# Per-tile first K and Q groups, small weights first on a second ring, and a landing margin for weight pieces, in a one-core attention and gated-MLP kernel

## The chip, the core and the metric

The kernel runs on one core of a Trainium2 chip. The metric is device time in microseconds (us) of one execution. Engines are called as in the profile: PE (matrix products; PEld is its loading of weights), ACT (activations), DVE (vector work), POOL, and SP, which here only issues DMA transfers. ACT can issue transfers too; the transfers of SP and of ACT go through two rings to the same 16 DMA engines.

## The reference

One transformer block on x of 2048 tokens by 1024 features, bf16:

```python
h  = x + A(layernorm(x))       # attention: 32 query heads of 32, one shared K and V head
h2 = h + B(layernorm(h))       # gated MLP, inner width 3584
# A: q = x@wq (1024x1024), k = x@wk, v = x@wv (1024x32 each)
#    o = softmax(q k^T / sqrt(32)) v ; o @ wo (1024x1024)
# B: (sigmoid(x@w_gate) * (x@w_up)) @ w_down
```

## The kernel before, in words

**A plan written at build time.** Every instruction is an `Op` (L22) with an engine, dependencies, a planned occupation and latency and a priority. `Plan` (L39 to L121) is a list scheduler: for each of ACT, DVE, POOL and SP it keeps a heap and a time `free`, and puts the ready op of best priority next (`step`, L79). A transfer (an op with `nbytes`) is planned to start 1.4 us after its issue or when the one before it has ended, to move 280 bytes per ns, and to land 0.9 us later (L99 to L102). PE's order is made by the main loop (L974 to L1044), which looks at the planned time `t` and chooses among score blocks, PV blocks and groups in `queues`, in the order of `PRIO` (L388). The plan's times exist only at build time; what is left in the program is the order of each engine's instructions, with semaphore waits. An engine that waits for one instruction holds up all behind it. The launch line and the helpers stand in several rows of the profile: L391 is every matrix product, L282 and L283 are copies out of PSUM on ACT and DVE.

**Stages.** 16 tiles of 128 tokens. x is loaded by SP (`load_x`, L296), pairs of tiles get their layer norm on DVE and POOL (`stats`, L326; centring L371, scaling L378), and the result is transposed: tiles 0 and 1 on PE (`mk_xT`, L417, copied out by ACT), the others by transposing transfers on SP (`dma_xT`, L439). From the transposed tiles PE makes K and V (`mk_KV`, L467) for each pair of tiles, and Q (`mk_Q`, L503) for each of 8 groups of 128 columns. K's weights are first repeated four times across columns by ACT (`rep_ops`, L322), so that K comes out in four row groups. w_k and w_v are loaded by ACT's ring (L311, L312), after x of tile 1 has landed in the plan. Q of the first two tiles goes to `QTb`; Q of the others goes through DRAM and comes back a tile at a time.

**Attention.** A *visit* (G, kq) is one pair of Q groups for one query tile (G counts them, four to a tile) against 256 keys (kq, 0 to 7). `emit_S` (L608) issues 8 score products into the PSUM tile `S_ps` (six banks, three pairs used in turn), and ACT takes exp of them in two instructions of 1024 columns (L631). The order is the list `visits` (L571 to L573): for the first four G in pairs of G through kq 0 to 3, then kq 4 to 7, then G by G. Each visit takes two of the 20 slots `Pr` (four of which lie in `wo_sb`); they come free once the PV block of four visits (`mk_PV`, L680) is done. PV, sums of the exponentials (L665, DVE) and the output projection (`mk_OP`, L788) follow.

**MLP.** For every tile: second layer norm, a transposing transfer of `hn` to `hnT` (L818), 14 gate and up groups (`mk_GU`, L880, 8 products of 512 columns each), tanh on ACT, product on DVE, a transposing transfer to `hact` (L917), and two down groups of 28 products (`mk_D`, L932). Gate and up weights don't fit: they are streamed in *pieces* of 256 KB (`load_piece`, L862) into 22 slots `ring`, again for every tile, with slots still held being reused. `pump` (L264) releases pieces to SP no faster than `PACE` bytes per ns once visit 120 is passed. A group is started only when its pieces are issued and, in the plan, its first two have landed (L926, L927).

**Filling.** Before the first visit PE runs products of the identity with zeros into `S_ps` bank 5 (L1034) to keep busy; later, when nothing is ready, products of `ident` with `kT4` (L1041), which show as F_ps<-kT,ident.

Of the kernel before, what the change touches and what calls it, by code (L numbers as in the profile page):

```python
# [13 lines left out]
P = 128  # L14
DH = 32
LN_EPS_BF16 = 1.0013580322265625e-05
SEM = 75.0
AHEAD = 200.0
PMAX = 1


# [17 lines left out]
class Plan:  # L39
# [3 lines left out]

    def __init__(self):
        self.lists = {e: [] for e in ("pe",) + self.ENG}
        self.free = {e: 0.0 for e in ("pe",) + self.ENG}
        self.heap = {e: [] for e in self.ENG}
        self.dma_free = collections.Counter()
        self.seq = 0
# [29 lines left out]
    def step(self, limit):  # L79
        best = None  # L80
        for e in self.ENG:
            h = self.heap[e]
            if h:
                s = max(self.free[e], min(o.ready for o in h))
                if best is None or s < best[0]:
                    best = (s, e)
        if best is None or (limit is not None and best[0] > limit):
            return False
        s, e = best
        h = self.heap[e]  # L90
        o = min((o for o in h if o.ready <= s + 1e-9), key=lambda o: (o.prio, o.seq))
        if e == "dve" and o.prio >= 3:
            soon = [x for x in h if x.prio <= PMAX and s < x.ready <= s + AHEAD]
            if soon:
                o = min(soon, key=lambda x: x.ready)
                s = o.ready
        h.remove(o)
        self.free[e] = s + o.occ
        if o.nbytes:  # L99
            go = max(s + 1400.0, self.dma_free["sp"])  # L100
            self.dma_free["sp"] = go + o.nbytes / 280.0
            o.end = self.dma_free["sp"] + 900.0  # L102
        else:
            o.end = s + o.lat
        o.pos = len(self.lists[e])
        self.lists[e].append(o)
        for u in o.users:
            u.ready = max(u.ready, o.end)
            u.missing -= 1
            if u.missing == 0:  # L110
                self.heap[u.eng].append(u)
        o.users = []
        return True
# [18 lines left out]
def t_mm(n):  # L132
    return dict(occ=max(25.0, n / 2.4 + 2.7), lat=max(25.0, n / 2.4 + 2.7) + 170.0 + SEM)


def bass_sequential_preLN__grouped_kv_mqa__glu_gated_glu__prompt_kernel(
# [12 lines left out]
    Bsz, S, D = A_x.shape  # L149
# [25 lines left out]
    DPP = 2  # L175
    NPI = DT // DPP
    USES = [(p, w, d) for t, p, w in ITEMS for d in range(NPI)]
    PACE = 205.0
    xf = A_x[0]
    of = out[0]  # L180

    with ExitStack() as es:
# [43 lines left out]
        def xnT(dt, a, n):  # L226
            return xnT4[a // 512][:, dt, a % 512:a % 512 + n]
# [24 lines left out]
        def dma(fn, key, nbytes, deps=(), prio=5, ring="sp", occ=520.0):  # L252
            return pl.op(ring, fn, deps, occ=occ, key=key, nbytes=nbytes, prio=prio)
# [19 lines left out]
        def evac(fn_act, fn_dve, n, deps, prio, dve_rate=0.96):  # L273
            now = pl.free["pe"]
            a = max(pl.free["act"], now) + sum(o.occ for o in pl.heap["act"]) + n / 1.2
            d = max(pl.free["dve"], now) + sum(o.occ for o in pl.heap["dve"]) + n / dve_rate
            if a + (2000.0 if v else 0.0) < d:
                return pl.op("act", fn_act, deps, prio=prio, **t_act(n))
            return pl.op("dve", fn_dve, deps, prio=prio, **t_dve(n, dve_rate))

        def both(out_ap, in_ap):
            return (lambda: ACT.activation(out=out_ap, in_=in_ap, func=ACTF.Copy),  # L282
                    lambda: DVE.tensor_copy(out=out_ap, in_=in_ap))  # L283
# [12 lines left out]
        def load_x(ts, deps=()):  # L296
            sl = slice(ts[0] * P, (ts[-1] + 1) * P)
            o = dma(lambda: SP.dma_start(x_sb[:, ts[0]:ts[-1] + 1, :], xf[sl, :].rearrange("(a p) n -> p a n", p=P)),
                    f"x{ts[0]}", P * D * 2 * len(ts), deps, prio=0)
            for t in ts:  # L300
                x_ld[t] = o

        def load_wq(a, b, deps=()):
            o = dma(lambda: SP.dma_start(wq2[a // 4][:, :, a % 4 * P:(a % 4 + b - a) * P], A_wq[:, a * P:b * P].rearrange("(a p) n -> p a n", p=P)),
                    f"wq{a}", D * P * (b - a) * 2, deps, prio=0)
            for g in range(a, b):
                wq_ld[g] = o

        load_x([0])
        load_x([1])  # L310
        wk_ld = dma(lambda: ACT.dma_start(wk_sb, A_wk.rearrange("(a p) j -> p a j", p=P)), "wk", P * DT * DH * 6, [x_ld[1]], prio=0, ring="act")  # L311
        wv_ld = dma(lambda: ACT.dma_start(wv_sb, A_wv.rearrange("(a p) j -> p a j", p=P)), "wv", P * DT * DH * 6, [x_ld[1]], prio=0, ring="act")  # L312
        load_wq(0, 2)
        load_x([2, 3])
        load_wq(2, 4)
        load_x([4, 5])
        warm = pl.op("act", lambda: ACT.activation(out=tnh[:, 0, 0:1], in_=half, func=ACTF.Exp), [c0], prio=1, occ=1400)

# [41 lines left out]
        xnorm = {}  # L360
        xT_ev = {}
        SCALE_ON = ["dve"] * 16
        for ts in [[t, t + 1] for t in range(0, NT, 2)]:
            sv = stats(0, ts, [x_sb[:, t, :] for t in ts], [[x_ld[t]] for t in ts], 3)
            if ts[0] + 6 < NT:
                load_x([ts[0] + 6, ts[0] + 7], [sv[2]])
            if ts[0] == 0:
                load_wq(4, 8, [sv[2]])
            for t in ts:
                xt, sc = x_sb[:, t, :], rstd[:, 0, t:t + 1]  # L370
                cen = pl.op("dve", lambda t=t, xt=xt: DVE.tensor_scalar(  # L371
                    out=xt, in0=xt, scalar1=mvr[:, 0, t, 0:1], scalar2=None, op0=ALU.subtract),
                    [sv[0]], prio=2, occ=360, lat=560)
                if SCALE_ON[t] == "act":
                    xnorm[t] = pl.op("act", lambda xt=xt, sc=sc: ACT.activation(out=xt, in_=xt, func=ACTF.Copy, scale=sc),
                                     [cen, sv[1]], prio=1, **t_act(1024))
                else:
                    xnorm[t] = pl.op("dve", lambda xt=xt, sc=sc: DVE.tensor_scalar(  # L378
                        out=xt, in0=xt, scalar1=sc, scalar2=None, op0=ALU.mult), [cen, sv[1]], prio=1, occ=360, lat=560)
# [5 lines left out]
                self.cls, self.atoms, self.first, self.after = cls, atoms, first, after  # L385

        queues = collections.defaultdict(collections.deque)
        PRIO = ["xT", "KV", "Q0", "OP", "GU", "D", "Q"]  # L388

        def mm(o, l, r, start, stop, **kw):  # L390
            fn = lambda: PE.matmul(o, lhsT=l, rhs=r, start=start, stop=stop, **kw)  # L391
            if not kw:
                fn.col = lambda: [mm(o[DH * j:DH * (j + 1)], l[:, DH * j:DH * (j + 1)], r, start, stop,
                                     tile_position=(0, DH * j)) for j in range(4)]
            return fn
# [48 lines left out]
            queue_after_xT(t)  # L444

        def queue_after_xT(t):
            if t % 2 == 1:
                for part in (("k", "v") if t == 1 else ("kv",)):
                    queues["KV"].append(mk_KV(t // 2, part))
            if t == 1:  # L450
                for g in range(NG):
                    queues["Q0"].append(mk_Q(g, 0, 256))
            if 1 < t < 8 and t % 2 == 1:
                for g in range(NG):
                    queues["Q"].append(mk_Q(g, (t - 1) * P, 256))
            if t % 4 == 3 and t > 8:
                for g in range(NG):
                    queues["Q"].append(mk_Q(g, (t // 4) * 512, 512))

        k_ev, v_ev = {}, {}  # L460

        q_left = [6 * NG]
        q_left4 = [2 * NG, 2 * NG, NG, NG]
# [104 lines left out]

        tile_last_S = {}

        visits = [(G + i, kq) for G in range(0, NX, 2) for kq in range(VPH) for i in range(2)]  # L571
        visits += [(G, kq) for G in range(NX) for kq in range(VPH, VPG)]
        visits += [(G, kq) for G in range(NX, NT * ND) for kq in range(VPG)]  # L573
        NV = len(visits)
# [8 lines left out]
        def s_ready(v):  # L583
            G, kq = visits[v]
            qb, g = G // ND, 2 * (G % ND)
            if any(g + k not in q_ready[qb] for k in range(2)):
                return None
            if kq not in k_ev:
                return None
            reclaim(v)  # L590
            if len(p_free) < 2:
                return None
            deps = [q_ready[qb][g], q_ready[qb][g + 1], k_ev[kq]]
            if 2 * v - 2 >= 0:
                deps.append(exps[2 * v - 2])
            return deps

        def reclaim(v):
# [375 lines left out]
        while True:  # L974
# [56 lines left out]
            if v == NV and cur is None and not any(queues.values()):  # L1031
                break
            if v == 0 and known([c_id, c_w], t):
                pl.op("pe", mm(S_ps[:, 5, :], ident[:, :], hact[:, 0:512], True, True), [c_id, c_w],  # L1034
                      **t_mm(512 if t > 5200.0 else 1024))
                continue
            idle += 1
            spare = [b for b in range(2) if known(bank_rel[b], t) and (cur is None or b != cur_b)]
# [112 lines left out]
```

The softmax here doesn't subtract the row's maximum and nothing guards it: scores larger than these inputs give would overflow.

## Time and profile before

| what | us |
|---|---|
| median of 7 runs | 1095.05 (1092.92 to 1097.06) |
| the profiled execution, its own time | 1093.38 |
| its span in the profile | 1091.3 |
| PE, ACT, DVE busy in it | 1049.5, 1006.3, 903.8 |
| first exp starts | 18.98 |
| last exp ends | 1022.2 |
| last product on PE | 1088.4 |

A row of the timeline reads: start, length, engine, line, operation, what it writes <- what it reads, shape, count, and in brackets the idle time of the engine before it and what ended it. A row of the page's list of groups ends with the busy time and the mean of one. A row of waits reads: engine, its line, who released it: us in total, times, longest. All durations come from this one profiled execution.

### The profile page before, as it was taken

Reading aid. Unit: us, or ns where it says so; the run is one execution under the profiler, and the core shown is the slowest. Engines: PE = TensorE matmul, PEld = TensorE weight load, DVE = VectorE, ACT = ScalarE, POOL = GpSimd, SP = SyncE. Lnnn points to the kernel's source line nnn. Section 1 sums busy time; section 2 is a strip of 40 time slices with the busy share of each in tenths; the row PEclk is TensorE's granted clock in tenths of the full one; section 3 lists DMA queues with packets and bytes.
Section 4 is the critical chain, followed back from the end, with each engine's and each line's share of the span. In section 5 each row is a group of like instructions: output and inputs, shape, how many; then the busy total and the mean of one; then the engine's idle time right before and its main releaser. Section 6 shows DMA issues by size and latency. Waiting matters only on the chain.

```text
span 1091.3 us, 31052 instructions
## 1 busy us (share of the span) xinstructions
PE 1049.5 (96%) x12601; PEld 480.0 (44%) x12775; DVE 903.8 (83%) x1755; ACT 1006.3 (92%) x1162; POOL 22.8 (2%) x56
## 2 busy tenths in 40 slices
PE   8999999999999999999999999999999999999998
PEld 5664444444444444444444444443444444444443
DVE  8779988898988988898988989898888989798711
ACT  4899999999999999999999999999999999999510
POOL 1100000000000000000000000000000000000000
PEclk9999999999999999999999999999999999999999
DMA  9896499959589696959789685969878595968993
GB/s 256 190 291 203 151 274 276 276 130 268 151 220 240 158 242 148 242 141 252 199 184 255 150 245 145 245 165 234 220 175 237 160 238 140 253 170 206 250 274 106
DMA packets 310990, 228.16 MB, mean 209 GB/s; under 512 B 121920, under 2 KB 302144, under 8 KB 310848
## 3 DMA queue, kind: packets, MB, share of 16 engines
q1 hardware_dynamic: 308768, 226.04, 80.4%
q8 instruction: 101, 1.65, 0.6%
q10 hardware_dynamic: 2080, 0.13, 0.1%
q14 instruction: 41, 0.34, 0.1%
HBM read 195.69 MB, written 7.86 MB: 187 GB/s over the span
## 4 chain that ended last, share of the span: by engine, by line
PE 63%; ACT 23%; issue 5%; DVE 5%; DMA 3%; ACTq 0%; SPq 0%; DVEq 0%
PE F_ps L391 54%; ACT Pr L631 22%; PE S_ps L391 10%; DVE Ts L665 3%; DMA zone<-in_A_wv_dram 1%; ACT tnh L909 1%; DMA ring<-in_B_w_up_dram 1%; DVE hst L913 1%; DVE Rc L727 1%; ACT wo_sb L631 1%; DMA zone<-ring 0%; DVE Rc L732 0%; DMA ring<-in_A_x_dram 0%; DVE Ri L730 0%; DVE Oc L715 0%
## 5 line engine op out<-in xcount | busy, mean ns | idle before, releaser
L631 ACT ACTIVATE Pr<-S_ps 128x1024 bf16<-128x1024 f32 x1014 | 961.7, 1178 | 5.5 <-PE S_ps L391 5.2
L665 DVE TENSOR_TENSOR Ts<-Ts,Pr 128x1024 bf16<-128x1024 bf16 x732 | 481.1, 678 | 45.7 <-ACT Pr L631 43.7
L391 PE MATMUL F_ps<-ring,hnT 128*128 128x512 bf16 (+1 forms) x1956 | 417.3, 380 | 19.1 <-issue 14.1
L391 PEld LDWEIGHTS F_ps<-ring,hnT 128*128 128x128 bf16 (+1 forms) x2045 | 155.6, 97 | 200.6 <-issue 55.6
L391 PE MATMUL F_ps<-zone,hact 128*128 128x512 bf16 (+1 forms) x1089 | 211.9, 380 | 6.7 <-issue 6.5
L391 PE MATMUL S_ps<-QTb,kT 32*128 32x256 bf16 x4096 | 203.3, 273 | 1.9 <-ACT wo_sb L631 0.8
L391 PEld LDWEIGHTS S_ps<-QTb,kT 32*128 32x128 bf16 x4096 | 60.6, 92 | 205.9 <-ACT Pr L631 161.6
L391 PE MATMUL F_ps<-Pr,Vb 128*32 128x256 bf16 x4056 | 134.5, 274 | 0.3 <-DVE Ts L665 0.3
L665 DVE TENSOR_TENSOR Ts<-Pr 128x1024 bf16<-128x1024 bf16 x126 | 85.9, 684 | 56.5 <-ACT Pr L631 56.3
L909 ACT ACTIVATE tnh<-F_ps 128x512 f32<-128x512 f32 x112 | 84.0, 750 | 47.7 <-PE F_ps L391 44.8
L391 PEld LDWEIGHTS F_ps<-zone,hact 128*128 128x128 bf16 (+1 forms) x1145 | 80.7, 97 | 97.7 <-issue 25.1
L391 PEld LDWEIGHTS F_ps<-Pr,Vb 128*32 128x32 bf16 x4056 | 96.8, 96 | 32.2 <-issue 18.8
L913 DVE SCALAR_TENSOR_TENSOR hst<-tnh,F_ps 128x512 bf16<-128x512 f32 x112 | 76.4, 682 | 26.7 <-PE F_ps L391 25.5
L391 PE MATMUL F_ps<-zone 128*128 128x256 bf16 (+4 forms) x603 | 73.9, 279 | 5.7 <-ACT QTb L282 1.5
L391 PE MATMUL F_ps<-wo_sb,OT 128*128 128x512 bf16 (+1 forms) x259 | 60.0, 380 | 3.1 <-issue 2.7
L391 PEld LDWEIGHTS F_ps<-zone 128*128 128x128 bf16 (+1 forms) x612 | 43.8, 97 | 28.6 <-issue 8.7
L672 DVE TENSOR_TENSOR Ts<-Ts 128x1024 bf16<-128x1024 bf16 x64 | 43.8, 684 | 0.6
L943 DVE SCALAR_TENSOR_TENSOR h_sb<-F_ps,h_sb 128x512 bf16<-128x512 f32 x32 | 21.9, 686 | 25.0 <-PE F_ps L391 25.0
L391 PEld LDWEIGHTS F_ps<-wo_sb,OT 128*128 128x128 bf16 (+1 forms) x277 | 21.5, 98 | 29.1 <-issue 7.1
L710 DVE COPY Oc<-F_ps 128x256 f32<-128x256 f32 x60 | 25.3, 422 | 4.2 <-PE F_ps L391 2.5
L715 DVE TENSOR_TENSOR Oc<-F_ps,Oc 128x256 f32<-128x256 f32 x60 | 25.4, 423 | 3.4 <-PE F_ps L391 2.2
L732 DVE STREAM_TRANSPOSE Rc<-Ri 128x256 f32<-128x256 f32 x64 | 28.1, 438 | 0.0
(60 smaller groups left out, 320.1 us busy)
## 6 DMA issues: line engine op xcount, KB each, us to landing
ring<-in_B_w_gate_dram SPq DMA_DIRECT2D x320, 256.0 KB, 4.0
ring<-in_B_w_up_dram SPq DMA_DIRECT2D x320, 256.0 KB, 3.9
zone<-in_B_w_down_dram SPq DMA_DIRECT2D x28, 256.0 KB, 3.9
h_sb<-in_A_x_dram SPq DMA_DIRECT2D x16, 256.0 KB, 4.5
out_dram<-h_sb SPq DMA_DIRECT2D x32, 128.0 KB, 3.0
ring<-in_A_x_dram SPq DMA_DIRECT2D x7, 512.0 KB, 7.0
QTb<-q_scratch SPq DMA_DIRECT2D x14, 256.0 KB, 3.8
q_scratch<-hact SPq DMA_DIRECT2D x16, 128.0 KB, 2.9
```

Of the source, the lines that this page charges most:

```text
L391: fn = lambda: PE.matmul(o, lhsT=l, rhs=r, start=start, stop=stop, **kw)
L631: exps[u] = pl.op("act", lambda slot=slot, pb=pb: ACT.activation(out=pslot(slot).rearrange("p (a b) -> p a b", a=2), in_=S_ps[:, pb:pb + 2 ...
L665: o = pl.op("dve", lambda T=T, a=a, b=b: DVE.tensor_tensor(out=T, in0=a, in1=b, op=ALU.add), deps, prio=4, **t_dve(1024, 1.92))
L672: merge_ev[G] = pl.op("dve", lambda T4=T4: DVE.tensor_tensor(out=T4[:, :, 0, :], in0=T4[:, :, 0, :], in1=T4[:, :, 1, :], op=ALU.add), [sum ...
L710: oc_ev[G] = pl.op("dve", lambda: DVE.tensor_copy(out=Oc[:, :], in_=O), [last, o_ev.get(G - 1)], prio=0, **t_dve(256))
L715: a = pl.op("dve", lambda: DVE.tensor_tensor(out=Oc[:, :], in0=O, in1=Ob, op=ALU.add), [last, oc_ev[G], o_ev.get(G - 1)], prio=0, **t_dve( ...
L727: c = pl.op("dve", lambda: DVE.transpose(out=Rc[:, :], in_=R), [last, o_ev.get(G - 1)], prio=0, **t_dve(256))
L732: d = pl.op("dve", lambda: DVE.transpose(out=Rc[:, :], in_=Ri[:, :].unsqueeze(2).to_broadcast([P, 2 * P // DH, DH])), [r], prio=2, **t_dve ...
L909: tanh_of[n] = pl.op("act", lambda: ACT.activation(out=tnh[:, n % 2, :], in_=F_ps[:, b, :], func=ACTF.Tanh, scale=0.5), [last, tn_user.get ...
L913: e = pl.op("dve", lambda: DVE.scalar_tensor_tensor(out=hst[:, n % NST, :], in0=tnh[:, n % 2, :], scalar=1.0, in1=F_ps[:, b, :], op0=ALU.a ...
L943: e = pl.op("dve", lambda: DVE.scalar_tensor_tensor(out=h_sb[:, t % 4, sl], in0=F_ps[:, b, :], scalar=0.5, in1=h_sb[:, t % 4, sl], op0=ALU ...
```

## The change

It alters the first twenty microseconds, the order of the first 16 visits, and three numbers of the plan.

- Tiles 0 and 1 get their statistics each by itself, in place of one pair.
- K and Q groups 0 and 1 of the first two tiles become one group H, in a class of its own: for each of the two tiles, three chains of 8 products of 128 columns, into bank 4 and bank 5 of `S_ps` and one bank of `F_ps`. The second visit waits until those banks are read. V of these tiles moves to the head of the queue of Q groups 2 to 7.
- w_k and w_v are issued by ACT first of all, waiting for nothing. The second half of w_q follows w_q's second quarter on SP, in place of waiting for the first statistics.
- The first visits take three G at key block 0 and 1, then two.
- Planned landing of weight pieces is 1.2 us later (`PIECE`), `PACE` goes from 205 to 245, and the plan's engines start at times above zero. The idle products go to bank 0, with another threshold for their planned length.

```diff
@@ -16,6 +16,7 @@
 LN_EPS_BF16 = 1.0013580322265625e-05
 SEM = 75.0
 AHEAD = 200.0
+PIECE = 1200.0
 PMAX = 1
 
 
@@ -43,7 +44,7 @@
 
     def __init__(self):
         self.lists = {e: [] for e in ("pe",) + self.ENG}
-        self.free = {e: 0.0 for e in ("pe",) + self.ENG}
+        self.free = {"pe": 650.0, "act": 700.0, "dve": 840.0, "pool": 720.0, "sp": 150.0}
         self.heap = {e: [] for e in self.ENG}
         self.dma_free = collections.Counter()
         self.seq = 0
@@ -99,7 +100,7 @@
         if o.nbytes:
             go = max(s + 1400.0, self.dma_free["sp"])
             self.dma_free["sp"] = go + o.nbytes / 280.0
-            o.end = self.dma_free["sp"] + 900.0
+            o.end = self.dma_free["sp"] + 900.0 + (PIECE if o.key.startswith("sl") else 0.0)
         else:
             o.end = s + o.lat
         o.pos = len(self.lists[e])
@@ -175,7 +176,7 @@
     DPP = 2
     NPI = DT // DPP
     USES = [(p, w, d) for t, p, w in ITEMS for d in range(NPI)]
-    PACE = 205.0
+    PACE = 245.0
     xf = A_x[0]
     of = out[0]
 
@@ -306,13 +307,16 @@
             for g in range(a, b):
                 wq_ld[g] = o
 
+        wk_ld = pl.op("act", lambda: ACT.dma_start(wk_sb, A_wk.rearrange("(a p) j -> p a j", p=P)), prio=0, key="wk",
+                      occ=450.0, lat=6200.0)
+        wv_ld = pl.op("act", lambda: ACT.dma_start(wv_sb, A_wv.rearrange("(a p) j -> p a j", p=P)), prio=0, key="wv",
+                      occ=450.0, lat=10200.0)
         load_x([0])
         load_x([1])
-        wk_ld = dma(lambda: ACT.dma_start(wk_sb, A_wk.rearrange("(a p) j -> p a j", p=P)), "wk", P * DT * DH * 6, [x_ld[1]], prio=0, ring="act")
-        wv_ld = dma(lambda: ACT.dma_start(wv_sb, A_wv.rearrange("(a p) j -> p a j", p=P)), "wv", P * DT * DH * 6, [x_ld[1]], prio=0, ring="act")
         load_wq(0, 2)
         load_x([2, 3])
         load_wq(2, 4)
+        load_wq(4, 8)
         load_x([4, 5])
         warm = pl.op("act", lambda: ACT.activation(out=tnh[:, 0, 0:1], in_=half, func=ACTF.Exp), [c0], prio=1, occ=1400)
 
@@ -360,12 +364,10 @@
         xnorm = {}
         xT_ev = {}
         SCALE_ON = ["dve"] * 16
-        for ts in [[t, t + 1] for t in range(0, NT, 2)]:
+        for ts in [[0], [1]] + [[t, t + 1] for t in range(2, NT, 2)]:
             sv = stats(0, ts, [x_sb[:, t, :] for t in ts], [[x_ld[t]] for t in ts], 3)
-            if ts[0] + 6 < NT:
-                load_x([ts[0] + 6, ts[0] + 7], [sv[2]])
-            if ts[0] == 0:
-                load_wq(4, 8, [sv[2]])
+            if ts[-1] % 2 and ts[-1] + 6 < NT:
+                load_x([ts[-1] + 5, ts[-1] + 6], [sv[2]])
             for t in ts:
                 xt, sc = x_sb[:, t, :], rstd[:, 0, t:t + 1]
                 cen = pl.op("dve", lambda t=t, xt=xt: DVE.tensor_scalar(
@@ -385,7 +387,7 @@
                 self.cls, self.atoms, self.first, self.after = cls, atoms, first, after
 
         queues = collections.defaultdict(collections.deque)
-        PRIO = ["xT", "KV", "Q0", "OP", "GU", "D", "Q"]
+        PRIO = ["xT", "H", "KV", "Q0", "OP", "GU", "D", "Q"]
 
         def mm(o, l, r, start, stop, **kw):
             fn = lambda: PE.matmul(o, lhsT=l, rhs=r, start=start, stop=stop, **kw)
@@ -444,11 +446,12 @@
             queue_after_xT(t)
 
         def queue_after_xT(t):
-            if t % 2 == 1:
-                for part in (("k", "v") if t == 1 else ("kv",)):
-                    queues["KV"].append(mk_KV(t // 2, part))
+            if t % 2 == 1 and t > 1:
+                queues["KV"].append(mk_KV(t // 2, "kv"))
             if t == 1:
-                for g in range(NG):
+                queues["H"].append(mk_H())
+                queues["Q0"].append(mk_KV(0, "v"))
+                for g in range(2, NG):
                     queues["Q0"].append(mk_Q(g, 0, 256))
             if 1 < t < 8 and t % 2 == 1:
                 for g in range(NG):
@@ -458,6 +461,39 @@
                     queues["Q"].append(mk_Q(g, (t // 4) * 512, 512))
 
         k_ev, v_ev = {}, {}
+        h_rel = []
+
+        def mk_H():
+            bank = [S_ps[:, 4, 0:256], S_ps[:, 5, 0:256], None]
+            w = [lambda dt: wk4[:, dt, :]] + [lambda dt, g=g: wq2[0][:, dt, g * P:(g + 1) * P] for g in range(2)]
+
+            def atoms(b):
+                out = bank[:2] + [F_ps[:, b, 0:256]]
+                r = []
+                for h in range(2):
+                    for i in range(3):
+                        for dt in range(DT):
+                            end = h == 1 and dt == DT - 1
+                            r.append((mm(out[i][:, h * P:(h + 1) * P], w[i](dt), xnT(dt, h * P, P), dt == 0, dt == DT - 1), P,
+                                      [xT_ev[h]] if dt == 0 else [], (lambda o, i=i: done(i, o, out[i])) if end else None))
+                return r
+
+            def done(i, last, src):
+                if i == 0:
+                    fa, fd = both(kT4[:, 0:256], src)
+                    k_ev[0] = evac(fa, fd, 256, [last], 1)
+                    h_rel.append(k_ev[0])
+                    return
+                q_left[0] -= 1
+                q_left4[0] -= 1
+                q_done[i - 1] += 256
+                fa, fd = both(QTb[:, :, i - 1, :], src.rearrange("p (a b) -> p a b", a=2))
+                q_ready[0][i - 1] = q_ready[1][i - 1] = evac(fa, fd, 256, [last], 1)
+                h_rel.append(q_ready[0][i - 1])
+
+            gr = Group("H", atoms, lambda: [xT_ev[0], rep_ops[-1], wq_ld[0], wq_ld[1]], lambda b, last: [h_rel[-1]])
+            gr.gate = lambda: not queues["xT"]
+            return gr
 
         q_left = [6 * NG]
         q_left4 = [2 * NG, 2 * NG, NG, NG]
@@ -568,7 +604,8 @@
 
         tile_last_S = {}
 
-        visits = [(G + i, kq) for G in range(0, NX, 2) for kq in range(VPH) for i in range(2)]
+        visits = [(0, 0), (1, 0), (2, 0), (0, 1), (1, 1), (2, 1), (0, 2), (1, 2), (0, 3), (1, 3),
+                  (2, 2), (3, 0), (2, 3), (3, 1), (3, 2), (3, 3)]
         visits += [(G, kq) for G in range(NX) for kq in range(VPH, VPG)]
         visits += [(G, kq) for G in range(NX, NT * ND) for kq in range(VPG)]
         NV = len(visits)
@@ -593,6 +630,8 @@
             deps = [q_ready[qb][g], q_ready[qb][g + 1], k_ev[kq]]
             if 2 * v - 2 >= 0:
                 deps.append(exps[2 * v - 2])
+            if v == 1:
+                deps += h_rel
             return deps
 
         def reclaim(v):
@@ -1031,8 +1070,8 @@
             if v == NV and cur is None and not any(queues.values()):
                 break
             if v == 0 and known([c_id, c_w], t):
-                pl.op("pe", mm(S_ps[:, 5, :], ident[:, :], hact[:, 0:512], True, True), [c_id, c_w],
-                      **t_mm(512 if t > 5200.0 else 1024))
+                pl.op("pe", mm(S_ps[:, 0, :], ident[:, :], hact[:, 0:512], True, True), [c_id, c_w],
+                      **t_mm(512 if t > 7000.0 else 1024))
                 continue
             idle += 1
             spare = [b for b in range(2) if known(bank_rel[b], t) and (cur is None or b != cur_b)]
```

## The prediction

> **What bounds the kernel now.** I read the page's header and busy slices first, then the busy times by stage, then the start and the end of the timeline, and the waits last.
>
> ```profile
> PE 1049.5 (96%) x12601; PEld 480.0 (44%) x12775; DVE 903.8 (83%) x1755; ACT 1006.3 (92%) x1162; POOL 22.8 (2%) x56
> ```
>
> Two engines are close to full, so it matters which of them the end hangs on. The stages say more (columns: stretch, its length, then busy us and instructions of PE, PEld, DVE, ACT, POOL; granted clock; DMA share; GB/s):
>
> ```profile
> 0.00:11.40 11.40, 9.68 (x50) 4.62 (x52) 7.52 (x19) 3.42 (x4) 2.04 (x10) 1.00 0.87 239
> ...
> 60.00:131.00 71.00, 67.96 (x978) 35.15 (x981) 67.47 (x138) 68.69 (x75) 1.51 (x2) 1.00 0.65 205
> 131.00:165.00 34.00, 32.78 (x388) 15.21 (x394) 30.16 (x56) 34.00 (x41) 0.00 (x0) 1.00 1.02 268
> 165.00:1022.00 857.00, 830.01 (x10158) 363.88 (x10308) 745.29 (x1408) 856.76 (x980) 11.76 (x28) 1.00 0.81 206
> 1022.00:1091.00 69.00, 65.71 (x366) 30.07 (x370) 17.04 (x32) 5.58 (x10) 0.79 (x2) 1.00 0.78 208
> ```
>
> From 131 to 1022 ACT never rests (exps back to back, 0.93 us apart). But after the last exp, at 1022.2, 69 us of PE work are left, and the tail shows whether they had to wait for anything:
>
> ```profile
> 1033.86 12.25 PE L391 MATMUL F_ps<-zone,hact 128*128 128x512 bf16 x55
> ...
> 1037.81 1.24 SPq L818 DMA_TRANSPOSE hnT<-hn  x1
> ...
> 1045.95 9.66 PE L391 MATMUL F_ps<-ring,hnT 128*128 128x512 bf16 x43
> ```
>
> The last tile's hnT is issued at 1037.8 and lands, at this kernel's 3 to 4 us, at about 1041.3. PE is on the down projection of the tile before until 1045.95 and has no gap. So PE, not ACT, sets the end, with about 4.7 us of slack for ACT. What counts is how much useful PE work is moved forward, or how much idle PE time goes; an exp that comes earlier alone gains nothing. The clock is 1.00 in every row and takes no part.
>
> Useful PE work starts late:
>
> ```profile
> 7.87 0.88 DVE L378 TENSOR_SCALAR ring<-ring,rstd 128x1024 bf16<-128x1024 bf16 x2
> ...
> 8.56 1.06 PE L420 MATMUL F_ps<-ident,ring 128*128 128x128 bf16 x16
> ...
> 11.40 1.91 PE L391 MATMUL F_ps<-zone 128*128 128x256 bf16 x16
> ...
> 14.00 1.33 ACT L322 ACTIVATE zone<-zone 128x256 bf16<-128x256 bf16 x4 [2.86 <-DMA zone<-in_A_wk_dram]
> ...
> 18.98 1.94 ACT L631 ACTIVATE Pr<-S_ps 128x1024 bf16<-128x1024 f32 x2 [0.56 <-PE S_ps L391]
> ...
> 25.68 2.20 PE L391 MATMUL F_ps<-zone 128*128 128x256 bf16 x31
> ```
>
> The first Q group waits for both tiles' transposes (11.40), K waits for w_k (14.00), so the first exp is at 18.98, and the first token pair's Q, K, V are only done when the second pair's K,V group starts at 25.68. From there PE is nearly gapless (Q work queued until 131). **The time at which the second pair starts is what I follow.**
>
> **First tiles apart, and H.** Today one statistics chain serves tiles 0 and 1: the cast (L340) starts at 6.17, the scale (L378) at 7.87, 1.7 us on. Split, tile 0's two bn_stats (3.35 to 4.64) lead to a cast at about 5.6 (one bn_stats of tile 1 slips between), scale 7.3. The ACT copy started 1.34 us after the scale (9.21 against 7.87): 8.65, plus 1.02, so xT0 is ready at 9.75. Tile 1: POOL's pow (0.90) runs after tile 0's, its scale at 8.3, its ACT copy behind the first, ready at 10.8. Price: two casts and a reciprocal on DVE (0.17+0.17+0.16=0.5 us) and 1.1 us on POOL, which is 98% idle. The DVE half microsecond is really paid only in 10 to 40 us, where DVE is full; it has waits of 0.42 and 0.65 us on x landings there (9.17, 12.82) that cover it. I book zero; without that cover 0.5.
>
> H is 48 matmuls of 128 columns in place of 24 of 256. The Trainium skill, "TensorE: Matmul & The Clock Gate", section "Back-to-back issue gap", speaks against it: a stream of weight load and matmul holds about 81 ns each at 128 columns. The row nearest, 16 transposes of 128 columns with their weight loads, took 1.06 us with 0.219 for the last: (1.06-0.219)/15 = 56 ns. By the row a half of H is 24x56 = 1.35 us, by the rule 1.94; the 256-wide ones ran at 1.91/16, about 113 ns, so by the row 48 narrow ones cost what 24 wide ones do. I take the row (same engine, shape and weight load): H from 9.8 to 11.15 and 11.15 to 12.5. K ends first (11.6), its copy 0.38 at 11.8, q0 and q1 behind on ACT until 13.1; scores, then first exp at 13.75: 5.2 us earlier. By the rule 14.4.
>
> **w_k, w_v first.** They take 0.42+1.18 us of ACT's queue ahead of the table load (1.28 us, now ending near 3.6; ACT has nothing before 8.6, so this is hidden). Again a rule speaks against it: the skill's "DMA: Bandwidth & Descriptors", section "Specifications", wants at least 512 B for line rate; these rows are 64 B.
>
> ```profile
> q10 hardware_dynamic: 2080, 0.13, 7.3%
> ```
>
> That is ACT's ring in the first 20 us: 0.073x16x20/2080 = 11.2 ns a packet, 1.46 us on each of 16 engines if all went ahead of x0. Interleaved with x0 (256 KB, landed at 3.35) far fewer do. Bounds 0 to 1.46, taken 0.3. Landing of w_k: it took 9.8 us when 2 MB of x and w_q shared the engines; started with them at 1.1 it has less beside it. Between 3.4 (as x0) and 11, I take 6.5: the four copies (1.33) end near 8, before xT0's copy. At 11 they would hold H back to 12.4, 2.6 us of the gain.
>
> **w_q's second half** (1 MB) goes ahead of x4,5 on SP instead of at 7.34. About 3.5 MB then lie ahead at about 290 GB/s: x4,5 land near 15 instead of 12.8, beside DVE's pair 1, which is done at 14.8. At most 1 us on pair 2. In return the transposes of tiles 2,3 find no w_q before them, and Q4 to Q7 have weights by 14.
>
> **Pair 2 start on PE.** x2,3 at 9.5; four bn_stats 2.5; small ops and 1.7 to the scale: 13.9; both scaled 14.8. Two transposes on SP took 3.46 us to issue (15.44); now from 14.5, the second at 16.2, landing 3.2 to 5.5 later: 19.4 to 21.7. PE meanwhile: V 0.5, six Q groups 5.6, three score blocks 1.5 from 12.5: 20.2. So 20.3 to 22; I take 21.2 against 25.68, **4.4 us**.
>
> **Visit order.** A third head pair at K0 fills ACT's hole between 24 and 28. But ten visits now take all 20 Pr slots, and the eleventh waits for the first PV (64 matmuls, 2.0 us): a hole of about 1.1 us in ACT, none before. It is inside ACT's slack: zero. Between 0 and 1.1.
>
> **Engine start offsets, warm-up bank, threshold.** They alter planned times and idle matmuls only: zero, plus or minus 0.3.
>
> **Landing margin and pace.** Pieces really take 3.9 to 4.0 us; the planner counts 1.4+0.94+0.9 = 3.2, so 1.2 covers it. What PE lost waiting for pieces:
>
> ```profile
> PEld F_ps L391 <- DMA ring<-in_B_w_up_dram: 1.9, 5, 0.6
> ...
> PEld F_ps L391 <- DMA ring<-in_B_w_gate_dram: 0.7, 1, 0.7
> ```
>
> With PE's own 0.9, some 3.5 us is the most there is to win. The cost: a group held 1.2 us is free while S, PV or D work is at hand, else filler. Fillers (kT,ident) are 32, about 3.5 us, nearly all at 148 to 178, where pieces are short (DMA 1.02). Pace 245 for 205 acts only after visit 120 (about 245 us). From -3.5 to +19 (1.2 in all 16 tiles); I take -0.6, nearer to the waits, since after 178 PE had no fillers.
>
> **Sum** -4.4 - 0.6 = -5.0. The profiled execution took 1093.38 (span 1091.3, 2.1 around it), so 1088.4 there; it was 1.67 below the median. From the median 1095.05: **1090.0**. Less than 0.2% (2.2 us) can't be told from no change.
>
> **Rivals.**
> - As summed, 1090.0, own range 1086.5 to 1092.5 (H and transposes each off by 1 to 2 us): 0.58.
> - The gain is given back, 1094.4: the stretch 131 to 178 is short of pieces, and if these arrive no earlier, PE reaches it 4.4 us sooner and fills. For: DMA 1.02 and the fillers. Against: DMA only 0.65 in 60 to 131, and the loads start on Q groups that move too. A w_k that lands late belongs here. 0.17.
> - Slower, 1099: the margin leaves PE without work in gate/up. At 1.2 us a tile, -4.4+1.2n passes +2.2 from n = 6 tiles; with 7, +4.0. For: PE sets the end, so each filler counts. Against: no fillers after 178. 0.17.
> - More, 1085.7: waits and half of the fillers go too, -4.4-3.4-1.6. 0.08.
>
> Range 1084.5 to 1097: it leaves out part of the first and last extremes. Faster 0.68, same 0.14, slower 0.18.
>
> **What would show it.** First exp near 13.75; w_k copies before 8.6; first K,V group of pair 2 near 21.2; last exp about 4 us earlier; the tail still gapless at 69 us or shorter. Wrong if the pair 2 group starts after 24, if fillers pass 40, or if PE has gaps after 1022.

## The result and the profile after

The changed kernel took 1091.45 us (median; 1090.35 to 1093.92) against 1094.71 for the kernel before, measured again beside it: a ratio of 0.9969 with a 95% interval of 0.9961 to 0.9978. That is 3.3 us (0.31%) faster; the forecast was 5.0 us from 1095.05. A second measurement, in the last set of experiments, gave 0.997 (0.9961 to 0.998). The two profiled executions differ by less, 1093.38 against 1091.78 (spans 1091.3 and 1089.5), since one execution scatters by 1 to 2 us; sizes of a microsecond or less that I read from the start and the end of a single one are rough. Some executions of either kernel have a granted clock of 0.997 or 0.998 and take 2 to 3 us longer, and leaving them out moves no ratio below by more than 0.0008.

The start of the timeline of the changed kernel answers to the lines of before:

```profile
4.40 1.33 ACT L326 ACTIVATE zone<-zone 128x256 bf16<-128x256 bf16 x4 [1.05 <-DMA zone<-in_A_wk_dram]
...
8.43 0.49 DVE L380 TENSOR_SCALAR ring<-ring,rstd 128x1024 bf16<-128x1024 bf16 x1
...
8.97 0.62 PE L422 MATMUL F_ps<-ident,ring 128*128 128x128 bf16 x8 [1.57 <-DVE ring L380]
...
10.95 1.06 PE L393 MATMUL S_ps<-zone 128*128 128x128 bf16 x16
...
15.01 1.94 ACT L670 ACTIVATE Pr<-S_ps 128x1024 bf16<-128x1024 f32 x2 [0.56 <-PE S_ps L393]
...
22.14 2.12 PE L393 MATMUL F_ps<-zone 128*128 128x256 bf16 x30
```

w_k's four copies by ACT start at 4.40 where they started at 14.00. H starts at 10.95, the first exp at 15.01 (before 18.98), and the second pair's K,V group, the milestone that the prediction followed, at 22.14 (before 25.68): 3.5 us earlier. The stages of 131 to 200 us and the end:

```profile
131.00:200.00 69.00, 66.93 (x777) 29.81 (x789) 61.11 (x115) 69.00 (x81) 1.58 (x2) 1.00 1.04 271
```

```profile
131.00:200.00 69.00, 65.40 (x833) 29.99 (x845) 60.58 (x115) 68.63 (x81) 0.81 (x2) 1.00 1.14 272
```

The first row is of the kernel before, the second of the changed one (columns as above: length, then busy us of PE, PEld, DVE, ACT, POOL; clock; DMA share; GB/s). In this stretch, where gate and up groups start, DMA moves the same 271 GB/s in both; PE got there about 3 us sooner (the first such group ran at 128.3 against 131.5) and is busy 1.5 us less. Products that only fill went from 29 to 36 between 120 and 200 us. The last exp and the tail:

```profile
1013.56 3.16 ACT L670 ACTIVATE Pr<-S_ps 128x1024 bf16<-128x1024 f32 x3
...
1033.65 1.25 SPq L857 DMA_TRANSPOSE hnT<-hn  x1
...
1038.07 9.66 PE L393 MATMUL F_ps<-ring,hnT 128*128 128x512 bf16 x43
...
1074.33 12.25 PE L393 MATMUL F_ps<-zone,hact 128*128 128x512 bf16 x55
```

The last exp ends at 1016.7, 5.5 us earlier, yet the last product ends at 1086.6, only 1.8 us earlier in these two executions. PE has no gap in the tail in either. The exps ran ahead and PE did not follow by as much: in the tail PE sets the end, as the prediction had it. Between the start and the tail it is ACT that sets the pace. From 241 to 1000 us, before and changed:

```profile
241.00:1000.00 759.00, 735.08 (x8988) 322.14 (x9119) 659.28 (x1245) 758.76 (x870) 9.39 (x24) 1.00 0.80 203
```

```profile
241.00:1000.00 759.00, 733.41 (x9163) 324.51 (x9293) 666.87 (x1247) 759.00 (x869) 14.29 (x24) 1.00 0.78 203
```

ACT is busy for 758.76 and 759.00 of 759 us, PE for 735 and 733. The last down group of a tile comes every 62.1 us in both, and it is no earlier in the changed kernel for tile 0 (its last row starts at 241.5 against 241.7). The lead of the early start sits in the exps, which are 5 to 6 us ahead from 50 us on, and it comes out only behind the last of them.

### The profile page after: what moved, and what is told of

It is laid out like the page before. It is cut to its first block, busy times and chain, and to the rows that moved or that the text cites. A ratio compares the mean times of both kernels' runs of the same rounds, so it can differ in the third digit from the quotient of the medians.

```text
span 1089.5 us, 31275 instructions
## 1 busy us (share of the span) xinstructions
PE 1046.3 (96%) x12757; PEld 481.2 (44%) x12931; DVE 910.4 (84%) x1756; ACT 1006.8 (92%) x1164; POOL 28.5 (3%) x58
## 3 DMA queue, kind: packets, MB, share of 16 engines
q10 hardware_dynamic: 2080, 0.13, 0.1%
## 4 chain that ended last, share of the span: by engine, by line
ACT 45%; PE 33%; issue 10%; DVE 10%; DMA 2%; POOL 0%; SPq 0%; DVEq 0%
ACT Pr L670 40%; PE F_ps L393 28%; ACT tnh L948 5%; DVE Ts L704 5%; PE S_ps L393 5%; DVE Rc L766 1%; DMA ring<-in_B_w_up_dram 1%; DVE h_sb L834 1%; DVE st L334 1%; DVE hact L284 1%; DVE Rc L771 0%; DMA zone<-ring 0%; DMA ring<-in_A_x_dram 0%; DVE Ri L769 0%; ACT wo_sb L670 0%
## 5 line engine op out<-in xcount | busy, mean ns | idle before, releaser
L393 PE MATMUL F_ps<-ring,hnT 128*128 128x512 bf16 (+1 forms) x2046 | 411.9, 380 | 19.2 <-issue 12.7
L948 ACT ACTIVATE tnh<-F_ps 128x512 f32<-128x512 f32 x112 | 86.4, 771 | 45.4 <-PE F_ps L393 45.4
L348 POOL TENSOR_SCALAR zb<-mvb 128x1 bf16<-128x1 bf16 (+1 forms) x25 | 11.2, 447 | 999.4 <-DVE mvb L344 999.4
```

What stands on the lines that cost most here:

```text
L348: f = pl.op("pool", lambda: POOL.tensor_scalar(out=zb[:, ph, sl].unsqueeze(2), in0=mvb[:, ph, sl, 1:2], scalar1=LN_EPS_BF16, scalar2=None, ...
L948: tanh_of[n] = pl.op("act", lambda: ACT.activation(out=tnh[:, n % 2, :], in_=F_ps[:, b, :], func=ACTF.Tanh, scale=0.5), [last, tn_user.get ...
```

## The experiments

After the result I held Theory 1: the start gives the gain, the shortage of pieces takes some back, and the plan's two numbers hardly matter. Its rivals were Theory 2 (the margin makes the fillers) and Theory 3 (the numbers give the gain).

### The start and the plan's numbers taken apart

**start_only**, changed kernel:

```diff
-PIECE = 1200.0
+PIECE = 0.0
-    PACE = 245.0
+    PACE = 205.0
```

> The changed kernel with the landing margin at 0 and the pace back at 205: the start alone. Theory 1 (the start gives all of it, and the shortage of pieces between 131 and 200 us takes part back whatever the plan's numbers): 1091 to 1092.5 us, second pair's K,V group near 22 us, fillers in 120 to 200 us about as many as in the changed kernel (33). Theory 2 (the margin itself makes the fillers and gives gain back): 1088.5 to 1090, fillers at most 28. Theory 3 (the numbers bring the gain, the start brings nothing that lasts): 1094 to 1095.

Measured 1098.32, ratio 1.0015 (1.0005 to 1.0026): slower than the kernel before. None of the three theories allowed this. (The 33 fillers of the expectation were miscounted; the changed kernel has 36, start_only 32.)

**no_margin**: only `PIECE = 0.0`.

> The changed kernel with the margin at 0, pace 245. Theory 1: within 0.7 us of the changed kernel (1091.5). Theory 2: 1088.5 to 1090, PE's waits for pieces longer but fillers down by 5 or more. Theory 3: 1093 or more, with longer waits for pieces in the steady state after 241 us.

Measured 1091.75, ratio 0.9952 (0.9936 to 0.9968).

**pace_205**: only `PACE = 205.0`.

> The changed kernel with the pace back at 205, margin kept. Theory 1: within 0.7 us of the changed kernel. Theory 2: the same as the changed kernel, since the margin is still there. Theory 3: 1093 or more if it is the pace that helps.

Measured 1094.14, ratio 0.9972 (0.996 to 0.9983).

**numbers_only**: the kernel before with both numbers.

> The kernel before with margin 1.2 us and pace 245 alone. Theory 1: 1094 to 1095.5, no change; fillers in 120 to 200 about 29 to 33. Theory 2: 1096 to 1097, with more fillers than the 29 of before. Theory 3: 1091.5 to 1092.5.

Measured 1095.69, ratio 0.9988 (0.9978 to 0.9997): some 1.3 us better, with an interval that ends just short of no change.

The kernel before took 1096.57 beside these four runs, so they are read by their ratios. With the early start one of the two numbers is needed, and the second adds nothing that can be told. Side by side the pace alone does better than the margin alone, 1091.75 against 1094.14. The start alone reaches the second pair just as early; PE's row in start_only:

```profile
22.00 1.15 PE L393 MATMUL F_ps<-zone 128*128 128x256 bf16 x13
```

It loses afterwards. I took the starts of the last DVE row that writes h_sb for the down groups of tile 0 and of tile 12, and divided by twelve tiles: before (987.0-241.7)/12 = 62.1 us a tile, changed kernel the same, no_margin 62.1, pace_205 62.2, start_only (993.2-240.4)/12 = 62.7. PE's longest waits in start_only between 241 and 1000 us, with the row of PEld that belongs to them, and then those of the kernel before in the same stretch, show one cause:

```profile
PE F_ps L393 <- issue: 14.0, 84, 0.6
PE F_ps L393 <- DMA ring<-in_B_w_gate_dram: 6.1, 12, 1.2
PE F_ps L393 <- DVE h_sb L834: 2.8, 11, 0.3
```

```profile
PEld F_ps L393 <- DMA ring<-in_B_w_gate_dram: 12.7, 20, 1.5
```

```profile
PE F_ps L391 <- issue: 19.3, 85, 0.6
PE F_ps L391 <- DVE Ts L665: 1.9, 12, 0.2
PE F_ps L391 <- DMA ring<-in_B_w_gate_dram: 0.5, 2, 0.3
```

The twelve waits on PE, 6.1 us in all, fall in ten of the twelve tiles, from 392 us on, about one tile apart. (PEld's waits lie in part under the same gaps, so the two rows are not to be added.) Tile by tile they fit the lost time: the first two of the twelve tiles have no such wait and take 62.1 us; the next ones have 0.85, 0.20, 0.42 and 1.22 us and are longer than 62.1 by 0.91, 0.13, 0.58 and 1.43. Over the twelve, 7.5 us are lost. The loss passes through ACT, which is short of score blocks then:

```profile
241.00:1000.00 759.00, 731.93 (x8796) 315.05 (x8926) 649.27 (x1232) 753.71 (x860) 10.31 (x24) 1.00 0.78 200
```

```profile
ACT Pr L670 <- PE S_ps L393: 4.4, 9, 0.6
```

The late pieces did not travel longer than others. They took 3.2 to 4.9 us from issue to landing (median 3.8), where all gate pieces of that stretch have a median of 4.2, the same as in the changed kernel. The plan counts on 3.2, and in this order PE reaches for these pieces some 3 to 4 us after their issue. With `PIECE` or with the faster pace PE's wait is 1.7 us (pace_205, 200 to 1000 us) or 0.2 us (no_margin). Theory 1 fell in its part on the numbers; I went on with Theory P: the start moves PE forward, and pieces that land late can eat that and more. Its rivals: Theory Q, that the start spoils PE's rhythm with or without pieces, and Theory R, that any change of the order moves the time this much.

### Pieces that are never late

**half_before** and **half_start**: the kernel before, and start_only, with

```diff
-                piece(sl), W[d * DPP * P:(d + 1) * DPP * P, p * FW:(p + 1) * FW]...
-                f"sl{sl}", P * DPP * FW * 2, ...
+                piece(sl)[:, 0:1, :], W[d * DPP * P:d * DPP * P + P, p * FW:(p + 1) * FW]...
+                f"sl{sl}", P * FW * 2, ...
...
-... piece(sl[d])[:, dt % DPP, :] ...
+... piece(sl[d])[:, 0, :] ...
```

> The kernel before, with every gate and up piece loaded only in its first 128 rows (128 KB, planned as such), which both products of a piece then use: it leaves out half of the gate and up weights, and PE's work is unchanged. No shortage of pieces. Theory P (pieces that land late are what spoils the start's gain): 1088 to 1092 us, some 4 us below the kernel before for fillers and waits at 131 to 200 us that go; it serves as the base for the next run. Theory Q (the start changes the rhythm of PE for the worse, pieces or not): the same for this run.

> The start alone (margin 0, pace 205) with pieces halved in the same way (half of the gate and up weights left out). Theory P: 3.5 us (2.5 to 4.5) below half_before, as the second pair's K,V group starts 3.5 us earlier and no wait for pieces is left; each tile of the steady state takes 62.1 us. Theory Q: no faster than half_before, tiles at 62.7 us as in start_only.

Measured 1092.29, ratio 0.9966 (0.9953 to 0.998), and 1087.44, ratio 0.9922 (0.9906 to 0.9938): the early start with the old numbers is now 4.9 us faster than its base, and neither run has a filler after 130 us. That is against Theory Q. The tiles of half_start take (981.6-236.5)/12 = 62.1 us, not 62.7. With the pieces' lateness gone, the same start that cost 1.7 us gains 4.9. The size is not clean, though. Half the loads also leave the DMA engines less busy for all else (116 GB/s in place of 203 from 241 to 1000 us), the planned order is another one, and in half_before two tiles lose 0.9 us each, one of them beside a late hnT. Four of half_before's twelve executions also have the lower clock; without them the gain is 4.2 us.

### Another order of the same work

**jit_before** and **jit_start**: the kernel before, and start_only, with

```diff
-SEM = 75.0
+SEM = 85.0
```

> The kernel before with the plan's semaphore delay at 85 ns in place of 75: nothing is altered but the planned order. It shows how much another order of the same work moves the time. Theory P: within 2 us of the kernel before, since its waits for pieces are only some 3.5 us in all. Theory R (any change of order moves the time by as much as the change measured, so that neither start nor numbers can be credited): 3 us or more off.

> The start alone (margin 0, pace 205) with the plan's semaphore delay at 85 ns. Theory P, if the late gate piece of each tile is a general effect of the early start: again about 1098 us with 0.5 us waits once a tile. Theory R: the wait once a tile is an accident of one order; 1091 to 1094 us, with few waits for pieces after 241 us.

Measured 1106.58, ratio 1.0091 (1.0069 to 1.0112), and 1103.6, ratio 1.007 (1.0053 to 1.0088). Both are far slower, at 62.8 and 62.9 us a tile, with PE waiting for gate pieces again (3.4 us in 9 waits and 5.2 us in 10). For the size of jit_before, Theory R is right and Theory P was wrong: one planned delay changed by 10 ns moves the time by 11 us, three times what the change did. For jit_start both missed. At this setting the early start is 3.0 us faster than the late one by the medians of five and four runs. Of the early start's three pairs with equal numbers and whole pieces, old numbers lose 1.7 us, SEM 85 gains 3.0, the change's own numbers gain about 2 (0.997/0.9988 = 0.998). So the sign of the start's worth depends on the order that follows, and its size has been seen in a few orders only. Late pieces are not all that SEM 85 costs: in jit_before, the third of the twelve tiles is 1.6 us longer without any wait for a piece. There PE stands idle for 1.5 us before 398.6, by the profile until DVE is done (L665), and ACT then lacks a score block for 1.3 us.

### Parts of the start

**no_h**: changed kernel without H, the loads still early.

```diff
-        for ts in [[0], [1]] + [[t, t + 1] for t in range(2, NT, 2)]:
+        for ts in [[t, t + 1] for t in range(0, NT, 2)]:
...
-            if t % 2 == 1 and t > 1:
-                queues["KV"].append(mk_KV(t // 2, "kv"))
+            if t % 2 == 1:
+                for part in (("k", "v") if t == 1 else ("kv",)):
+                    queues["KV"].append(mk_KV(t // 2, part))
...
-                queues["H"].append(mk_H())
-                queues["Q0"].append(mk_KV(0, "v"))
-                for g in range(2, NG):
+                for g in range(NG):
```

> The changed kernel with tiles 0 and 1 in one statistics pair again and K, V and Q groups of 256 columns as before; w_k, w_v and w_q's second half stay early, and so do the visit order, margin and pace. Theory P (the start's gain is the second pair's earlier K,V group, to which the early loads give part): second pair's group between 22 and 25.7 us, near 23.5; time 1 to 2 us above the changed kernel. Theory R (the time follows the plan's numbers and rhythm, the start is not what counts): within 0.7 us of the changed kernel.

Measured 1090.43, ratio 0.9957 (0.9945 to 0.997), beside 1091.97 for the changed kernel in the same set. Theory P's price for H was wrong: without H it is no slower. It is 1.5 us faster by the medians; the intervals of the ratios overlap, but its five runs (1089.74 to 1090.85) lie below eight of the changed kernel's nine (1090.32 to 1094.37). ACT's copy of the second pair's K, in no_h and in the changed kernel:

```profile
23.89 0.38 ACT L283 ACTIVATE kT<-F_ps 128x256 bf16<-128x256 f32 x1
```

```profile
23.60 0.38 ACT L283 ACTIVATE kT<-F_ps 128x256 bf16<-128x256 f32 x1 [0.23 <-PE F_ps L393]
```

It was at 27.14 before. Nearly all of its advance comes without H, whose own first exp is 1.7 us earlier (15.01 against 16.70).

**old_visits**: changed kernel with the first visits as before (the two lines of `visits` put back).

> The changed kernel with the first 16 visits in the order of before. Theory P (PE sets the end, ACT has slack): within 1 us of the changed kernel, with the last exp up to 4 us later. Theory S (the earlier exps of the third head pair are what brings the gain): 1093.5 us or more.

Measured 1092.82, ratio 0.9973 (0.9964 to 0.9983), beside 0.997 for the changed kernel. ACT's last exps in it:

```profile
1010.53 11.21 ACT L669 ACTIVATE Pr<-S_ps 128x1024 bf16<-128x1024 f32 x12
```

They end at 1021.7, where the changed kernel's end at 1016.7. Five microseconds on ACT cost 0.85 us by the medians, no more: this is the slack in the tail that the prediction gave it. Theory S is out.

**pace_280**: changed kernel with `PIECE = 0.0` and `PACE = 280.0`.

> The changed kernel with margin 0 and pace 280 in place of 245. If faster release of pieces is what removes the waits once a tile, it is as fast as with 245 and margin 0 (0.995 of the kernel before) or faster, waits for pieces after 241 us under 1 us. If pieces sent faster hold up other transfers, 1093 us or more with waits for hact or hnT.

Measured 1091.22, ratio 0.9968 (0.9956 to 0.998); PE has no wait for pieces after 241 us in its trace. A faster pace brings nothing over 245.

**after_again**, the changed kernel unaltered:

> The changed kernel itself, beside the three above on the same chip: 0.997 of the kernel before (0.996 to 0.998). All theories say the same; it is the base for the three.

Measured 1091.97, ratio 0.997 (0.9961 to 0.998).

Four kernels (the changed one, no_margin, no_h, pace_280) lie within 0.9952 to 0.997 with overlapping intervals. Only no_h stands out when it is set beside the changed kernel directly, by 1.5 us in one set of runs; the others are not shown to beat the change.

## Why the prediction was right, and where it was not

**PE sets the end.** Right for the tail, and shown: old_visits moves the last exp by 5 us and the time by less than 1. From 241 to 1000 us it is not the whole: there ACT is never idle in the two kernels and PE idles for 24 to 26 us, so what PE loses costs time when ACT runs out of score blocks.

**First exp 13.75, measured 15.01.** x0 landed 0.5 us later than before (first bn_stats at 3.87 against 3.35); I had taken 0.3 and then left it out of the chain. POOL's pow took 1.00 and not 0.90, with tile 1's first POOL step behind it. And the plan put a bn_stats of tile 2 ahead of tile 1's reciprocal, which started at 9.55 although pow had ended at 8.95. The size was off; H's own length was right by the row: its first 16 products took 1.06 us, as the 16 transposes did, so 56 ns each and not the 81 that the Trainium skill gives in "TensorE: Matmul & The Clock Gate", section "Back-to-back issue gap". (The 256-wide ones, 1.91/16, are 119 ns and not 113, which changes nothing.)

**w_k and w_v.** Weighing the row above the 512 bytes of the Trainium skill's "DMA: Bandwidth & Descriptors", section "Specifications", held: their ring, with its rows of 64 bytes, again took only 7.2% of the engines in the first 20 us, and w_k was in use at 4.40, sooner than the 6.5 that I took.

**Second pair: -4.4, measured -3.5** (22.14 against 21.2). The cause that I gave was partly wrong: I worked it out through H, but no_h has the group as early. Nor is it the order of the visits: old_visits has the group at 22.17. What is left is mainly the early loads; which of them I did not separate, nor the planned start times of the engines.

**"From -3.5 to +19; I take -0.6, nearer to the waits".** This is the step that failed. I added the two numbers as a term of their own and sized them by the waits that the profile of before shows. But those waits belong to the order of before, and even there they were not a price. (The sum of 3.5 also counts in part twice, since PE's waits and PEld's lie under the same gaps.) The kernel before has its two PE waits for gate pieces, 0.3 and 0.2 us, in the first of the twelve tiles; ACT is not idle there and the tile takes its 62.1 us. A start that is 3.5 us earlier gives another order for all that follows, and in that order a gate piece is late in ten of twelve tiles, in most of them by enough to reach ACT. Margin and pace together are worth about 1.3 us on the old start, and on the new one either alone is worth 4.7 to 7 us (1.0015 to 0.9972, 1.0015 to 0.9952). So the sum came near the result with some luck: neither of its two terms was right by itself, and they were not independent.

**The rivals.** The second one, the gain given back where pieces are short, is seen in part: between 120 and 200 us PE's idle time rose from 2.4 to 4.5 us and its fillers from 29 to 36 (4.3 to 4.9 us) in the profiled executions, and without shortage the start gained 4.9 us rather than 3.3. The intervals of the two are too wide to call the difference shown. The third, that the margin leaves PE without work, did not happen: no filler after 200 us, and the run without margin is no more than 2 us faster by its ratio. Slower came from the other side, too little margin.

Open: why the plan puts PE at just those pieces so early after the early start with the old numbers, which of the early loads brings the second pair forward, and most of the 11 us of SEM 85. With times that move by 11 us when the order changes, the 3.3 us are shown for this kernel, not for the idea of an early start.

## What to carry to other kernels

Where a planner writes the order of the whole program, a gain at the start is kept only if what follows is still in time: look at the time per tile in the steady state, at the engine that is never idle there, and at waits that come back every tile, before crediting or blaming the part that was edited. A transfer planned to land a microsecond too early costs nothing in one order and half a microsecond in most tiles of another, so price a margin against what it insures, not against today's waits. And take away one part at a time: the most elaborate part of this change, H with its split of the first tiles, brought a first exp 1.7 us earlier and no time at the end.

## What the runs showed of the hardware that was not expected

A load of 64 KB in rows of 64 bytes (w_k), issued first on a ring of its own, was in use 3.7 us after its issue (0.72 to 4.40). The same load took 9.8 us to land in the kernel before, where it was issued at 4.15 and went beside transfers of 512 KB and 1 MB on the other ring. Packets on its ring take only 11 ns each (7.2% of 16 engines over 20 us, 2080 packets), so its place in the order mattered more than its size.

A wait of PE has no fixed price. In start_only, waits for gate pieces of 0.2 to 1.2 us lengthened their tiles by 0.1 to 1.4 us, because ACT, busy for 753.71 of 759 us, ran out of work. In the kernel before, two such waits of 0.2 and 0.3 us cost their tile nothing.
